# A transformer block in one core: when GpSimd sums the second weight set, in the first half of the feed-forward part

## The chip, the core and the metric

The kernel runs on one core of a Trainium2 chip. The metric is the device time of one launch in microseconds (us). The core has five engines, each with its own instruction queue that is worked off in order: TensorE (PE in the profile; PEld is its weight load, which overlaps with matmuls), VectorE (DVE), ScalarE (ACT), GpSimd (POOL) and SyncE (SP), which here only issues transfers. Engines wait for each other on semaphores. ScalarE issues transfers too.

## The reference

A block with adaptive layer norm: an attention part (32 heads of 18, four segments of 512 rows with a memory), then a feed-forward part. The change lies in the latter:

```python
h = _layernorm(x, axis=-1) * (1 + cb) + sb          # x: 2048 x 576
x = x + gb * _B_ref(h, B_w_gate, B_w_up, B_w_down)

def _B_ref(x, w_gate, w_up, w_down):                # 576 x 4608, 576 x 4608, 4608 x 576
    g = _silu(x @ w_gate)
    u = x @ w_up
    return (g * u) @ w_down
```

All in float32.

## The kernel before

The attention part takes up to some 660 us and is not touched. The feed-forward part runs in two halves, `t = 0` and `t = 1`, of 1024 rows each. In each half a loop goes over 18 pairs `p` of weight blocks (2 x 128 of the 4608 columns). Each pair has two sets `z`: 0 is gate, 1 is up. A set's product of a 2 x 2 block of operands is made from seven products instead of eight (sums and differences of blocks; `m` = 1 to 7), so a pair has 14 steps `k` (0 to 13), one product each. A product is seven float32r matmuls of 512 columns: operands are split in a high part (`wh`, a cast on ScalarE) and a low part (`wl`, the difference, on VectorE). The list of steps is `ZM`; the last product of a set, `m = 3`, stands in step 1 of the next set (k = 8 for gate, k = 1 of the next pair for up).

The order of instructions on every engine is the order in which the program records them (a manual schedule); tiles bring the waits. In one step the recording order is: casts of weights to come (`prep_w`), the splits on VectorE that belong to the casts of the step before (`later`), the product with what follows it (`step`, which calls `fin`), loads, casts of the 64-row remainder (`prep_r`), GpSimd's sums and products, stores, down-projection work, the cast of down weights (`prep_d`) and of activations (`prep_a`).

- **Weights.** `load_o` brings a set `O[p, z]` of 768 KB (first half) to one of two buffers. Four of its seven blocks must first be made by `sum_o`: four GpSimd instructions of 128 x 384. `prep_w` runs five products ahead (`PF = 5`), with nine buffers. In the first half `store_o` writes the four sums to DRAM, and the second half loads them ready made, so GpSimd has no work there.
- **Remainder.** `prep_r(0, p, z, part)` casts the remainder of three blocks (`part` 0) and of the four summed ones (`part` 1); `store_r` keeps it for the second half.
- **Down weights.** `load_d` brings 576 columns for two blocks to one buffer, `mul_d` multiplies them with `gbB` (two GpSimd instructions), `sum_d` makes four differences for the second half (GpSimd), `prep_d` casts, and a store to `wdD` at k = 12 frees the buffer.
- **Products' ends.** Bank A is written by m = 1, 6, 7 and 4 in turn, each adding to the last, so ScalarE's copies (to bank B, to `tb`, to `tc`) must be made before the next product on it. `fin` ends a block of the result: VectorE adds `tb` or `tc` to the bank (L1150 for gate, L1158 for up), ScalarE takes the silu (L1151, or L1148 straight from the bank), and the up set multiplies (L1155, L1159). `tb` and `tc` have one buffer each.
- **Down projection.** In the first half, `plain` adds one chunk of the pair before (12 matmuls of 288 columns into `pd`, two buffers) in each of the steps 4 to 11, and VectorE adds `pd` to the accumulator (L1260).
- **The second block's preparation.** In steps 2 to 11 of the first half a generator (`g2`, `prep2`) makes the other 1024 rows' operands, with small transfers on SP, casts on ScalarE and a few instructions on VectorE and GpSimd.

Per step of the first half, the touched order before: the load of the next pair's set 0 at k = 2 and of its set 1 at k = 12; `sum_o` of set 0 at k = 7, 8, 9, of set 1 in the next pair at k = 2, 3, 4; `mul_d` at k = 5, 6; `sum_d` at k = 6, 7, 9, 10.

Of the kernel before, what the change touches and what calls it, by code (L numbers as in the profile page):

```python
# [34 lines left out]
PF = 5  # L35
# [39 lines left out]
def block(ctx: ExitStack, tc: tile.TileContext, x, wqk, wv, wo, beta, wgu, wd, c, w_mod, out):  # L75
    nc = tc.nc
# [997 lines left out]
    def store_o(p, z):  # L1074
        nc.scalar.dma_start(oD[p][z], O[p, z][:, 3:7, 0:2])

    def prep_r(t, p, z, part=0):
        if part == 0:
            R[z] = wrp.tile([P, 7, P], F32R, tag="wr", name="wr")
        r = R[z]  # L1080
        if t == 1:
            (nc.sync if p or z == 0 else nc.scalar).dma_start(f32(r[0:96]), rD[p][z])
            return
        o, c = O[p, z], slice(0, 3) if part == 0 else slice(3, 7)
        nc.scalar.copy(r[0:96, c], o[0:96, c, 2, :])
        later.append(lambda: nc.vector.tensor_tensor(r[32:64, c], o[32:64, c, 2, :], f32(r[32:64, c]), op=ALU.subtract))

    def sum_o(p, z, j):
        o = O[p, z]
        d, a, b, op = ((4, 3, 2, ALU.add), (5, 4, 0, ALU.subtract), (3, 0, 3, ALU.subtract), (6, 1, 5, ALU.subtract))[j]  # L1090
        nc.gpsimd.tensor_tensor(o[:, d], o[:, a], o[:, b], op=op)  # L1091

    def store_r(p, z):
        nc.scalar.dma_start(rD[p][z], f32(R[z][0:96]))
# [17 lines left out]
    def mul_d(p, f):  # L1112
        v = RW[p][:, 2 * f:2 * f + 2].rearrange("p a b -> p (a b)")
        nc.gpsimd.tensor_tensor(v, v, gbB, op=ALU.mult)

    def sum_d(p, j):
        r = RW[p]
        d, a, b = ((4, 1, 0), (5, 3, 4), (6, 2, 5), (1, 3, 1))[j]
        nc.gpsimd.tensor_tensor(r[:, d], r[:, a], r[:, b], op=ALU.subtract)
# [17 lines left out]
                             skip_group_check=not first)  # L1137

    T, SG, AC, AP = {}, {}, {}, {}

    def tmp(tag, bufs=1):
        return tp.tile([P, L], F32, tag=tag, name=tag, bufs=bufs)

    def fin(z, ij, bank, add=None):
        if z == 0:
            SG[ij] = g = tmp("sg", NSG)
            if add is None:
                nc.scalar.activation(g, bank, AF.Silu)  # L1148
            else:
                nc.vector.tensor_tensor(g, bank, add, op=ALU.add)  # L1150
                nc.scalar.activation(g, g, AF.Silu)  # L1151
            return
        g = SG.pop(ij)
        if add is None:
            nc.vector.tensor_tensor(g, bank, g, op=ALU.mult)  # L1155
        else:
            u = tmp("cu", 2)
            nc.vector.tensor_tensor(u, bank, add, op=ALU.add)  # L1158
            nc.vector.tensor_tensor(g, u, g, op=ALU.mult)  # L1159
        AC[ij] = g  # L1160
# [114 lines left out]
    with tc.manual_schedule():  # L1275
# [101 lines left out]
        for t in range(2):  # L1377
            for p in range(NPR):
                last = t == 1 and p == NPR - 1
                nx = (p + 1) % NPR  # L1380
                tn = t if nx else t + 1
                if t == 0 and p == NPR - 1:
                    run(g2)
                    p6.close()
                    accq = pool(p4, "acq")
                    new_acc(accq, (1, 6, 7))
                if last:
                    load_x11(1)
                chunk = 0
                for k in range(14):  # L1390
                    z, m = ZM[k]
                    todo, later[:] = later[:], []
                    while nw < len(seq) and nw <= n + PF:
                        prep_w(*seq[nw])
                        nw += 1
                    n += 1
                    for f in todo:
                        f()
                    if k != 1 or prev is not None:
                        step(z, m)  # L1400
                    if k == 1 and prev is not None:
                        PA[0, 1] = AC[0, 1]
                    if t == 0 and p == NPR - 1 and k in (7, 9, 10, 11, 12, 13) or t == 1 and p == 0 and k == 1:
                        load_y(ACT_OP[m])
                    swap = t == 1 and p == 0
                    if not last and k == 7 - PF + swap:
                        load_o(tn, nx, 0)
                    elif not last and k == (14 - PF if tn else 12):
                        load_o(tn, nx, 1)
                    if t:  # L1410
                        if k == 2 + swap:
                            prep_r(1, p, 1)
                        elif not last and k == 9:
                            prep_r(1, nx, 0)
                    else:
                        if k in (3, 7):
                            prep_r(0, p, 1, k // 7)
                        elif tn == 0 and k in (9, 10):
                            prep_r(0, nx, 0, k - 9)
                        elif tn and k == 8:  # L1420
                            prep_r(1, 0, 0)
                        if k == 1:
                            load_d(0, p)
                        elif k in (2, 3, 4) and p:
                            for j in ((0, 1), (2,), (3,))[k - 2]:
                                sum_o(p, 1, j)
                        elif k in (5, 6):
                            mul_d(p, k - 5)
                        if tn == 0 and k in (7, 8, 9):
                            for j in ((0,), (1, 2), (3,))[k - 7]:  # L1430
                                sum_o(nx, 0, j)
                        if k in (6, 7, 9, 10) and p < NPR - 2:
                            sum_d(p, (6, 7, 9, 10).index(k))
                        if k == 0 and p == 0:
                            store_o(p, 0)
                        elif k == 3:
                            store_r(p, 0)
                        elif k == 6:
                            store_o(p, 1)
                        elif k == 10:  # L1440
                            store_r(p, 1)
                        elif k == 12:
                            nc.scalar.dma_start(wdD[p][:, :NS[p]], RW[p][:, :NS[p]])
                        elif k == 13 and tn == 0:
                            store_o(nx, 0)
                    if t and k == 2 + 2 * swap:
                        load_d(1, p)
                    if prev is not None and is_plain(*prev):
                        if k in (0, 2):
                            ij = (1, 0) if k == 0 else (0, 1)  # L1450
                            prep_a(prev[1] % 2, ij, PA[ij])
                        if CH0[t][k]:
                            f = plain(*prev, chunk)
                            if f:
                                late[k + 3] = f
                            chunk += 1
                        due(k)
                    elif prev is not None:
                        for j in range(4):
                            if k == KS[j]:  # L1460
                                sum_a(j)
                        if k == 0:
                            prep_a(prev[1] % 2, 2, PA[1, 0])
                        for j, kk in KA:
                            if k == kk:
                                prep_a(prev[1] % 2, j, PA[ASRC[j]])
                        for _ in range(CH[k]):
                            down(*prev, chunk)
                            chunk += 1
                    if last and 1 <= k < 9:  # L1470
                        comb(k - 1)
                    if p == 0 and (t, k) in RS:
                        load_res(t, RS[t, k])
                    if is_plain(t, p):
                        if k in (6, 7, 8, 10):
                            j = (6, 7, 8, 10).index(k)
                            prep_d(p, (j // 2, j % 2), j)
                    elif k >= 7:
                        prep_d(p, POS[k - 7], WSLOT[POS[k - 7]])
                    for ij, kk, j in (((0, 0), 11, 1), ((1, 1), 13, 4)):  # L1480
                        if k == kk:
                            prep_a(p % 2, ij if is_plain(t, p) else j, AC[ij])
                    if t == 0 and k in G2 and p > 0:
                        next(g2, None)
                for k in sorted(late):
                    due(k)
                PA.clear()
                PA.update(AC)
                prev = (t, p)
# [61 lines left out]
```

## Time and profile before

| | us |
|---|---|
| median of 3 runs | 1945.05 (1944.93 to 1948.55) |
| the profiled execution | 1944.18 |
| its span, first to last instruction | 1942.5 |
| TensorE busy | 1884.8 |
| VectorE busy | 1522.1 |
| ScalarE busy | 925.9 |
| GpSimd busy | 581.8 |

The prediction shows the profile's lines. They are read so: a window's row has start and end, length, then the busy time and the instructions of each engine, the granted clock of TensorE as a share of full speed, and the transfers. A group's row has the line, engine, operation, output and inputs, shape, count, busy time, mean in ns of one, and the idle time of the engine before them with what ended it. A row of waits has who waited for whom, the total, the number of times and the longest. A row of the timeline has start, length, engine, line, operation and count; in brackets stands idle time before it.

### The profile page before, as it was taken

To read this page: it belongs to the slowest core of one execution; us is meant where nothing else is said; L and a number is where in the kernel's file an instruction comes from. 1 tells how busy PE (TensorE), PEld (TensorE's weight loads), DVE (VectorE), ACT (ScalarE), POOL (GpSimd) and SP (SyncE) were. 2 spreads that over 40 slices of the span, in tenths; PEclk is the share of its full clock that TensorE was granted. 3 is DMA by queue.
4 is the path that set the end of the run, shared out by engine and by line. 5 is a ranking of instruction groups with operands and counts; after the bars stand their busy time and mean duration, and the time that the engine had idled before them with its cause. 6 is when DMAs were issued, how large, how long until landed. Compare 5 with 4: busy or idle time off the path is not lost.

```text
span 1942.5 us, 30570 instructions
## 1 busy us (share of the span) xinstructions
PE 1884.8 (97%) x10927; PEld 1568.8 (81%) x10927; DVE 1522.1 (78%) x3267; ACT 925.9 (48%) x2036; POOL 581.8 (30%) x772
## 2 busy tenths in 40 slices
PE   7999999999999799999999999999999999999999
PEld 4888865676766688888888888888888888888888
DVE  6485257878786899898778889876888888888887
ACT  2222256767666444444444444443444445454442
POOL 5222235555544645454345445310000000000000
PEclk9999999999999899999999999999999999999999
DMA  7767565444444555454445454369323333332331
GB/s 207 240 224 244 201 204 145 127 144 145 137 128 125 167 197 176 132 196 157 153 163 168 151 171 154 113 227 292 112 81 117 100 121 100 113 108 86 110 108 63
DMA packets 173543, 296.63 MB, mean 153 GB/s; under 512 B 25104, under 2 KB 101776, under 8 KB 171920
## 3 DMA queue, kind: packets, MB, share of 16 engines
q1 hardware_dynamic: 143280, 237.09, 39.0%
q10 hardware_dynamic: 30112, 57.60, 8.5%
q8 instruction: 86, 1.41, 0.3%
q14 instruction: 65, 0.53, 0.1%
HBM read 185.29 MB, written 109.31 MB: 152 GB/s over the span
## 4 chain that ended last, share of the span: by engine, by line
PE 84%; DVE 7%; DMA 5%; issue 1%; ACT 1%; POOL 1%; SPq 0%; ACTq 0%; DVEq 0%; POOLq 0%
PE A L1136 22%; PE pd L1256 13%; PE C L1136 10%; PE pd L1239 9%; PE B L1136 5%; PE pp L101 5%; PE s L589 4%; PE av L609 4%; PE s L187 4%; PE pv L101 3%; PE pw L707 2%; DVE wl L1101 1%; DMA mD<-mr 1%; DVE al L1200 1%; DVE y L938 1%
## 5 line engine op out<-in xcount | busy, mean ns | idle before, releaser
L1136 PE MATMUL A<-y,wh 128*128 128x512 f32 x1152 | 408.6, 395 | 10.1 <-ACT tb L1164 7.8
L192 DVE CUSTOM_DVE_ANT_0 junk<-s,tri 128x256 bf16<-128x256 f32 (+3 forms) x512 | 228.6, 487 | 76.5 <-PE s L187 67.9
L1101 DVE TENSOR_TENSOR wl<-O,wh 128x256 fp32r<-128x256 f32 x504 | 271.4, 540 | 5.4 <-ACT wh L1100 4.8
L1136 PEld LDWEIGHTS A<-y,wh 128*128 128x128 f32 x1152 | 217.7, 189 | 57.5 <-ACT tb L1164 11.0
L1091 POOL TENSOR_TENSOR O<-O 128x384 f32<-128x384 f32 x144 | 167.7, 1181 | 223.4 <-DMA O<-in_wgu_dram 75.0
L592 ACT ACTIVATE Pt<-s 128x512 f32<-128x512 f32 (+1 forms) x352 | 186.6, 558 | 87.3 <-PE s L589 72.7
L1136 PE MATMUL A<-y,wl 128*128 128x512 f32 x576 | 227.7, 395 | 0.0
L1244 DVE TENSOR_TENSOR acc<-acc,pd 128x576 f32<-128x576 f32 x216 | 162.3, 751 | 55.1 <-PE pd L1239 48.0
L1100 ACT CAST wh<-O 128x256 fp32r<-128x256 f32 x504 | 198.5, 404 | 11.5 <-DMA O<-in_wgu_dram 10.8
L1136 PE MATMUL C<-y,wh 128*128 128x512 f32 x576 | 202.5, 392 | 0.0
L1260 DVE TENSOR_TENSOR acc<-acc,pd 128x576 f32<-128x576 f32 x156 | 117.2, 751 | 98.6 <-PE pd L1256 97.9
L1256 PE MATMUL pd<-dh,ah 128*128 128x288 f32 x640 | 190.1, 297 | 4.3 <-DVE acc L1260 4.1
L1256 PE MATMUL pd<-dh,al 128*128 128x288 f32 x640 | 189.7, 296 | 0.0
L1256 PE MATMUL pd<-dl,ah 128*128 128x288 f32 x640 | 189.6, 296 | 0.0
L1200 DVE TENSOR_TENSOR al<-sg,ah 128x512 fp32r<-128x512 f32 x192 | 152.1, 792 | 12.1 <-ACT ah L1199 11.6
L1199 ACT CAST ah<-sg 128x512 fp32r<-128x512 f32 x192 | 118.7, 618 | 81.3 <-DVE sg L1159 79.6
L589 PE MATMUL s<-qs,ks 110*128 110x512 f32 (+2 forms) x384 | 149.8, 407 | 6.2 <-DMA qs<-mD 3.8
L1151 ACT ACTIVATE sg<-sg 128x512 f32<-128x512 f32 x73 | 46.2, 633 | 222.1 <-DVE sg L1150 222.1
L187 PE MATMUL s<-ks,qs 108*128 108x256 f32 (+3 forms) x512 | 141.3, 327 | 2.8 <-DMA ks<-kD 1.4
L1239 PE MATMUL pd<-dh,ah 128*128 128x288 f32 x448 | 133.0, 297 | 0.0
L1239 PE MATMUL pd<-dh,al 128*128 128x288 f32 x448 | 132.5, 296 | 0.0
L1239 PE MATMUL pd<-dl,ah 128*128 128x288 f32 x448 | 132.3, 295 | 0.0
(349 smaller groups left out, 4458.9 us busy)
## 6 DMA issues: line engine op xcount, KB each, us to landing
O<-in_wgu_dram SPq DMA_DIRECT2D x36, 768.0 KB
oD<-O ACTq DMA_DIRECT2D x36, 512.0 KB
O<-oD SPq DMA_DIRECT2D x36, 512.0 KB
ks<-kD SPq DMA_DIRECT2D x68, 216.0 KB
qs<-qD SPq DMA_DIRECT2D x68, 216.0 KB
O<-in_wgu_dram SPq DMA_DIRECT2D x36, 384.0 KB
rD<-wr ACTq DMA_DIRECT2D x36, 336.0 KB
wr<-rD SPq DMA_DIRECT2D x35, 336.0 KB
```

The lines of the kernel that those rows point to most:

```text
L187: nc.tensor.matmul(bank[:, n * (h - h0):n * (h - h0) + n], lhsT=qst[b][0:108, h, 128 * i:128 * i + 128], rhs=kst[b][0:108, h // 2, 0:n], s ...
L192: nc.vector.tensor_tensor_reduce(junk[:, :n], bank[:, n * (h - h0):n * (h - h0) + n], tri[:, L - n:], 1.0, -3e38, op0=ALU.add, op1=ALU.max ...
L589: nc.tensor.matmul(bank[:, n * (g - h):n * (g - h + w)].rearrange("p (a b) -> p a b", a=w), lhsT=kst[u % NB][0:110, g // 2, 128 * j:128 * ...
L592: nc.scalar.activation(pt[:, h:h + per, :n], bank[:, :n * per].rearrange("p (a b) -> p a b", a=per), AF.Exp, scale=SCALE)
L1091: nc.gpsimd.tensor_tensor(o[:, d], o[:, a], o[:, b], op=op)
L1100: nc.scalar.copy(wh, o)
L1101: later.append(lambda: nc.vector.tensor_tensor(wl, o, f32(wh), op=ALU.subtract))
L1136: nc.tensor.matmul(bank, lhsT=a, rhs=b, start=(first and n == 0), stop=(n == 6), skip_group_check=not first)
L1200: later.append(lambda: nc.vector.tensor_tensor(al, src, f32(ah), op=ALU.subtract))
L1239: nc.tensor.matmul(pd[:, i, :288], lhsT=a[:, tk], rhs=w, start=(k == 0), stop=(k == 2))
L1244: nc.vector.tensor_tensor(o, o, pd[:, :, :288], op=ALU.add)
L1256: nc.tensor.matmul(pd[:, i, :288], lhsT=a[:, tk], rhs=w, start=(k == 0), stop=(k == 5))
```

## The change

Five things move; no instruction is added or taken away.

1. The silu of L1151 is put off: it is recorded in the next step, behind that step's casts of weights and splits. This holds in both halves.
2. First half: the load of the next pair's set 1 moves from k = 12 to k = 8 (in the change's words, which count from 1: step 9). For this, step 7 casts two products' weights and step 8 none.
3. First half: set 1's sums move from k = 2, 3, 4 of their own pair to k = 10 and 11 of the pair before, two each; set 0's go from k = 7, 8, 9 to k = 4 to 7, one each.
4. `mul_d` goes one step earlier (k = 4, 5), `sum_d` stands at k = 6, 7, 8, 9, the first three `prep_d` one step earlier, and the second `prep_r` of set 1 at k = 5 and not 7.
5. Stores: the sums of set 0 at k = 11 (was 13), those of set 1 at k = 13 (was 6 of the next pair), the remainder of set 1 at k = 8 (was 10). Pair 0 stores both sets' sums at k = 0.

```diff
@@ fin
                 nc.vector.tensor_tensor(g, bank, add, op=ALU.add)
-                nc.scalar.activation(g, g, AF.Silu)
+                acts.append(lambda: nc.scalar.activation(g, g, AF.Silu))
@@ the loop over steps
-                    while nw < len(seq) and nw <= n + PF:
+                    while nw < len(seq) and nw <= n + PF + (t == 0 and k == 7):
                         prep_w(*seq[nw])
                         nw += 1
                     n += 1
                     for f in todo:
                         f()
+                    while acts:
+                        acts.pop(0)()
...
                     if not last and k == 7 - PF + swap:
                         load_o(tn, nx, 0)
-                    elif not last and k == (14 - PF if tn else 12):
+                    elif not last and k == (14 - PF if tn else 8):
                         load_o(tn, nx, 1)
...
-                        if k in (3, 7):
-                            prep_r(0, p, 1, k // 7)
+                        if k in (3, 5):
+                            prep_r(0, p, 1, k // 5)
...
                         if k == 1:
                             load_d(0, p)
-                        elif k in (2, 3, 4) and p:
-                            for j in ((0, 1), (2,), (3,))[k - 2]:
-                                sum_o(p, 1, j)
-                        elif k in (5, 6):
-                            mul_d(p, k - 5)
-                        if tn == 0 and k in (7, 8, 9):
-                            for j in ((0,), (1, 2), (3,))[k - 7]:
-                                sum_o(nx, 0, j)
-                        if k in (6, 7, 9, 10) and p < NPR - 2:
-                            sum_d(p, (6, 7, 9, 10).index(k))
+                        elif k in (4, 5):
+                            mul_d(p, k - 4)
+                        if tn == 0 and 4 <= k < 8:
+                            sum_o(nx, 0, k - 4)
+                        elif tn == 0 and k in (10, 11):
+                            sum_o(nx, 1, 2 * k - 20)
+                            sum_o(nx, 1, 2 * k - 19)
+                        if k in (6, 7, 8, 9) and p < NPR - 2:
+                            sum_d(p, k - 6)
                         if k == 0 and p == 0:
                             store_o(p, 0)
+                            store_o(p, 1)
                         elif k == 3:
                             store_r(p, 0)
-                        elif k == 6:
-                            store_o(p, 1)
-                        elif k == 10:
+                        elif k == 8:
                             store_r(p, 1)
+                        elif k == 11 and tn == 0:
+                            store_o(nx, 0)
                         elif k == 12:
                             nc.scalar.dma_start(wdD[p][:, :NS[p]], RW[p][:, :NS[p]])
                         elif k == 13 and tn == 0:
-                            store_o(nx, 0)
+                            store_o(nx, 1)
...
                     if is_plain(t, p):
-                        if k in (6, 7, 8, 10):
-                            j = (6, 7, 8, 10).index(k)
+                        if k in (5, 6, 7, 10):
+                            j = (5, 6, 7, 10).index(k)
                             prep_d(p, (j // 2, j % 2), j)
```

More of the change, by code (lines that the diff above doesn't have):

```diff
@@ L1139, in block @@
     T, SG, AC, AP = {}, {}, {}, {}
+    acts = []
     def tmp(tag, bufs=1):
```

## The prediction

> **What bounds the kernel now.** I read the page first, for the engine that is full, then the first half of the feed-forward part pair by pair, then who holds the matmuls up there, then the chain through one such hold.
>
> ```profile
> span 1942.5 us, 30570 instructions
> ...
> PE 1884.8 (97%) x10927; PEld 1568.8 (81%) x10927; DVE 1522.1 (78%) x3267; ACT 925.9 (48%) x2036; POOL 581.8 (30%) x772
> ```
>
> TensorE is busy for 97% of the span, and the change removes no matmul. All it can win is time in which TensorE stands still, or runs at half clock, in the part it touches. The next view cuts that part (659.7 to 1308.8 us) into its 18 pairs of weight blocks; I show a quiet one, the three worst and the sum.
>
> ```profile
> core 0: us, PE busy (x) PEld busy (x) DVE busy (x) ACT busy (x) POOL busy (x), PEclk, DMA share, GB/s
> ...
> 936.80:975.60 38.80, 36.41 (x203) 31.97 (x202) 29.27 (x44) 17.43 (x39) 18.16 (x17) 1.00 0.47 148
> 975.60:1015.20 39.60, 37.36 (x196) 32.37 (x195) 31.13 (x49) 17.15 (x41) 13.40 (x13) 0.96 0.40 129
> ...
> 1087.00:1122.40 35.40, 35.40 (x195) 31.17 (x194) 31.66 (x46) 16.40 (x39) 18.24 (x16) 1.00 0.55 165
> ...
> 1232.60:1273.40 40.80, 37.42 (x196) 32.30 (x195) 34.74 (x48) 16.79 (x41) 13.95 (x13) 0.96 0.41 132
> ...
> sum 649.10, PE 635.79 PEld 554.62 DVE 543.94 ACT 299.05 POOL 296.69; mean PE 35.32 PEld 30.81 DVE 30.22 ACT 16.61 POOL 16.48
> ```
>
> A quiet pair takes 35.4 us, with TensorE busy throughout. Three pairs take 3.4 to 5.4 us more. Over all 18 TensorE idles 649.1 - 635.8 = 13.3 us, and in two of the three bad pairs the granted clock falls to 0.96: 0.04 x 39.6 and 0.04 x 40.8, so 1.6 us each. The prize is thus about 16.5 us, under 1%. Who holds TensorE there, and after 1309 us:
>
> ```profile
> PE A L1136 <- ACT tb L1164: 7.8, 6, 2.4
> PE pd L1256 <- DVE acc L1260: 4.1, 2, 3.4
> PE A L1136 <- ACT cu L1164: 0.7, 1, 0.7
> PE pt L1036 <- DVE acc L1260: 0.5, 1, 0.5
> ```
>
> ```profile
> PE A L1136 <- DMA y<-yD: 1.5, 1, 1.5
> ```
>
> Mostly it is the copy of `tb` on ScalarE, which must clear bank A before the next product adds to it. The second half has no wait but one on a transfer. The chain through the hold at 943 us says what makes the copy late:
>
> ```profile
> 930.69 1.63 PE A L1136 x7
> 932.32 1.62 PE pd L1256 x12
> ...
> 935.31 1.42 DVE al L1200
> ...
> 939.92 1.34 DVE wl L1101
> 941.26 1.84 DVE al L1200
> ...
> 944.65 0.61 DVE cu L1158
> ...
> 945.36 0.59 ACT tb L1164
> ```
>
> The rows also give the steps (I count `k` from 0, as the loop does): 1.6 us for a product, 1.6 us more in steps 4 to 11, which carry down-projection work. So steps 12, 13 and 0 to 3 are short, 9.7 us for six, and steps 4 to 11 are long, 8 x 3.2 = 25.7 us. The chain runs through VectorE in the short steps: `cu` frees the one `tb` buffer, and stands behind `wl` and `al` that take 1.3 to 1.8 us. GpSimd is at work at that very time:
>
> ```profile
> 934.00 5.04 POOL L1091 TENSOR_TENSOR O<-O 128x384 f32<-128x384 f32 x4 [7.72 <-DVE dl L1126]
> 939.55 3.01 POOL L1114 TENSOR_TENSOR dr__11734<-dr__11734,gbB 128x576 f32<-128x576 f32 x2 [0.52 <-DMA dr__11734<-in_wd_dram]
> 942.51 1.25 POOL L1119 TENSOR_TENSOR dr__11734<-dr__11734 128x288 f32<-128x288 f32 x1
> ```
>
> That GpSimd makes VectorE slow is seen by comparing the first half (first fence, 684 to 1309 us) with the second, where GpSimd does nothing:
>
> ```profile
> L1101 DVE TENSOR_TENSOR wl<-O,wh 128x256 fp32r<-128x256 f32 x239 | 158.7, 667 | 2.8 <-ACT wh L1100 2.3
> L1260 DVE TENSOR_TENSOR acc<-acc,pd 128x576 f32<-128x576 f32 x136 | 102.1, 751 | 81.3 <-PE pd L1256 80.6
> L1200 DVE TENSOR_TENSOR al<-sg,ah 128x512 fp32r<-128x512 f32 x69 | 67.7, 981 | 3.9 <-ACT ah L1199 3.4
> L1086 DVE TENSOR_TENSOR wr<-O,wr 32x384 fp32r<-32x384 f32 x66 | 52.3, 793 | 2.5 <-ACT wr L1085 0.5
> ...
> L1158 DVE TENSOR_TENSOR cu<-C,tb 128x512 f32<-128x512 f32 x17 | 11.6, 680 | 0.0
> ```
>
> ```profile
> L1101 DVE TENSOR_TENSOR wl<-O,wh 128x256 fp32r<-128x256 f32 x224 | 93.7, 418 | 0.0
> L1200 DVE TENSOR_TENSOR al<-sg,ah 128x512 fp32r<-128x512 f32 x112 | 76.8, 686 | 4.4 <-ACT ah L1199 4.4
> ...
> L1126 DVE TENSOR_TENSOR dl<-dr__18260,dh 128x288 fp32r<-128x288 f32 x7 | 3.2, 453 | 0.0
> ```
>
> `wl` has a mean of 667 ns against 418, `al` 981 against 686. Last, the short steps at the start of a pair in which GpSimd happened to be almost idle, and at that of two bad ones:
>
> ```profile
> 717.80:727.49 9.69, 9.69 (x45) 7.96 (x44) 9.24 (x18) 4.02 (x10) 1.02 (x1) 1.00 0.91 320
> ...
> 933.57:945.80 12.23, 10.04 (x45) 7.92 (x43) 11.77 (x13) 3.90 (x10) 9.18 (x7) 1.00 0.46 165
> 972.40:984.99 12.59, 10.35 (x46) 7.95 (x45) 12.10 (x14) 4.08 (x11) 8.91 (x8) 1.00 0.46 162
> ```
>
> Even with GpSimd idle VectorE is busy 9.24 of 9.69 us there: it has no room. With 9 us of GpSimd work, one of its instructions takes 0.86 to 0.91 us instead of 0.51, and TensorE pays.
>
> **The change part by part.** *The second set's load and sums.* Today the load of the next pair's second set stands on SP's queue behind all transfers of steps up to 11, and behind the last split of the buffer it overwrites. It starts late:
>
> ```profile
> 720.11 0.91 SPq L1069 DMA_DIRECT2D O<-in_wgu_dram  x1
> ```
>
> ```profile
> 726.33 0.41 ACT L1100 CAST wh<-O 128x256 fp32r<-128x256 f32 x1 [1.85 <-DMA O<-in_wgu_dram]
> ```
>
> That one was issued in step 13 (717.80 is the start of step 12), and the cast of step 2 waited for it: 726.3 less 720.1 to 721.0 is 5.3 to 6.2 us of landing. With the last cast of the old set in step 7, its split in step 8, and the load in step 8 ahead of that step's other transfers, it lands by 5.3 to 6.2 us, so in step 10. The four sums (5.04 us in the row above) then run in steps 10 and 11 and not in 12 to 4. Nothing queues behind the load on SP but small transfers of the second block's preparation. On GpSimd only such work of steps 10 and 11 queues behind the sums.
>
> *The first set's sums and the products with `gbB`.* The multiply comes first (step 4), then the sums alternate with the rest in steps 4 to 9. The first sum waits for the load issued in step 2 or 3, which by the same 5.3 to 6.2 us lands in step 5, and now has the second multiply behind it. That one is needed by the cast of step 7, so the 6.4 us of steps 5 and 6 cover its 1.3 + 1.5 us. The first multiply may run from the landing of its weights, at 939.55 in the row above, which was step 1: about half of 3.01 us stays in the short steps, against some 9 us now. VectorE loses on it at the rate below 0.8 us, and has 0.4 us of room, so it is some 0.4 us late once a pair. I price that at nothing to 0.5 us a pair, and take 0.05, since pairs that carry more GpSimd work than that there show no wait.
>
> *What steps 4 to 11 then hold.* VectorE has 8 `wl` x 0.418, 8 evictions x 0.751, 4 `dl` x 0.453, 4 `wr` x at most 0.793 and 4 others x 0.68: 17.0 us of 25.7. GpSimd gets 18 less 1.6, about 16 us. What does a microsecond of GpSimd cost VectorE? From the short steps: (0.905 - 0.513) x 13 / 9.18 and (0.864 - 0.513) x 14 / 8.91, both 0.55. From the long steps of another pair:
>
> ```profile
> 1021.60:1047.00 25.40, 25.40 (x151) 22.95 (x150) 21.73 (x31) 11.51 (x27) 13.69 (x12) 1.00 0.48 150
> ```
>
> (21.73 - 17.0) / 13.69 = 0.35. I take 0.35, since it comes from the same steps: 17.0 + 5.6 = 22.6 of 25.7 us, and TensorE waits for nothing, as in that row. The other end, 0.55, makes 25.8, just full. So the work hides behind TensorE, and the cover ends at (25.7 - 17.0) / 16 = 0.54. The evictions, for which TensorE waits there, keep 751 ns in both cases, for one of their inputs is in PSUM.
>
> The Trainium skill (SBUF — State Buffer, "Who interferes with whom") has a rule that speaks against the move: a VectorE instruction with two SBUF inputs and a GpSimd one that reads SBUF exclude each other, and whichever starts second waits for the whole of the other. The rows agree on who suffers (`wl`, `al`) and who doesn't (the evictions, `cu`). By that rule alone the 16 splits of steps 4 to 11 could each wait up to one sum of 1.26 us, 20 us in all and 11 us a pair too many; with GpSimd there 62% of the time and half an instruction left on average it is 16 x 0.62 x 0.63 = 6.3 us, which fits again.
>
> *Silus one step later.* ScalarE stands in these silus now:
>
> ```profile
> ACT sg L1151 <- DVE sg L1150: 133.4, 37, 9.0
> ```
>
> The cast of the next step now goes first. The result is read in the second set's steps, seven or more later, so nothing waits for it. In the first pair, where the casts that stood between silu and `tb` copy (0.4 us each) get out of the way, 0.8 us of a 1.1 us wait goes. In the second half, where TensorE never waits for ScalarE, it costs nothing.
>
> *Casts of `wr` and `dh` earlier, an extra cast in step 7, stores moved.* As many instructions as before. ScalarE is busy 16 to 17 us of 35.4, and casts stand five steps (8 to 16 us) ahead of their product. The store of the second set in step 13 makes ScalarE wait for the sums; landing early in step 10 plus 5.0 us is the end of step 11, and a copy TensorE needs comes only in step 0. This costs nothing unless the load is 3 us late.
>
> *The sum.* Two of the waits on `tb` fall in pairs 0 and 1 (659.5 to 693 us):
>
> ```profile
> PE A L1136 <- ACT tb L1164: 2.1, 2, 1.1
> ```
>
> Of the 7.8 us I keep 1.0 (pair 1: pair 0 has no down work, so its steps are too short for load and sums to finish in time) and 0.3 in pair 0: gain 6.5, and 1.6 for the half clock at 985 us. The waits on evictions (4.6 us, and 1.6 of half clock) come from another cause:
>
> ```profile
> 1241.24 6.54 DVE L999 TENSOR_TENSOR st<-t,st 32x256 fp32r<-32x256 f32 x1
> ```
>
> GpSimd ran without a break there, and one VectorE instruction got no turn. That may happen again in the new order; I count half, 3.1. Less 16 x 0.05 = 0.8. Together 6.5 + 1.6 + 3.1 - 0.8 = 10.4 us. The profiled execution took 1944.18 us (1.7 beyond its span), 0.9 below the median: 1933.8, and 1934.6 by the median. I say 1934.
>
> **The rivals.** *Everything goes.* If the new order also gives every VectorE instruction its turn, all but the 0.7 us at the first copy is won: 13.3 - 0.7 + 3.2 = 15.8, so 1929. For it: quiet pairs have no wait at all. Against: the single 6.54 us stall.
>
> *The wait moves.* The load is on time, but the lag that VectorE collects in steps 10 and 11 reaches `cu` in step 1 after all, or the load still stands behind a transfer and the sums stay where they are. Then dense waits remain and the time is 1945. For it: the short steps have 0.4 us of room. Against: a lag of one sum is well below the one that nine us of GpSimd work makes.
>
> *Slower: steps 4 to 11 overflow.* One mechanism: GpSimd's unbroken row of work in steps 5 to 8 and 10 to 11 costs VectorE over 0.54 us per us, evictions come late, and TensorE waits for one of the two `pd` buffers. At 0.60, 17.0 + 9.6 = 26.6, 0.9 us too many in 16 pairs, 14 us, with no gain left: 1959. For it: 0.55 was measured, and the 6.54. The Trainium skill's rule from above leads here, if a sum always starts just ahead of a split. Against: the pair with 13.69 us of GpSimd in these steps, and none waiting.
>
> **How the numbers follow.** Forecast 0.50, everything goes 0.25, the wait moves 0.11, overflow 0.14. About 0.2% (3.9 us) is what can be told from no change here. So faster 0.75, same 0.11, slower 0.14. The range goes from 1927 (all waits, and what the pairs lose beside them) to 1946, which takes in the unmoved case and leaves out the overflow.
>
> **What would show it.** Right: sums of the second set in steps 10 and 11; no wait of bank A on `tb` beyond the first two pairs; pairs at 35.4 to 36 us; `al`, which falls in the short steps, back near 690 ns; the first half some 10 us shorter, and the second unchanged. Wrong: waits of `pd` on `acc` in many pairs (overflow), second-set sums after step 12, ScalarE standing in the store of step 13, or the clock falling in other pairs.

## The result and the profile after

| | before | after |
|---|---|---|
| median, us | 1945.85 (4 runs, 1944.93 to 1948.55) | 1928.95 (4 runs, 1926.12 to 1931.29) |
| ratio, 95% interval | | 0.991 (0.9893 to 0.9928) |
| the profiled execution | 1944.18 | 1926.12 |

The kernel is 16.9 us faster, 14 to 21 us by the interval. The profiled execution of after is the fastest of its four.

The page of after:

```profile
span 1924.3 us, 30622 instructions
...
PE 1874.0 (97%) x10927; PEld 1562.5 (81%) x10927; DVE 1512.8 (79%) x3267; ACT 929.8 (48%) x2036; POOL 581.0 (30%) x772
```

The 18 pairs of the first half, as windows; I show pair 1, the pairs that were the worst (8, 9 and 16), the quiet one (12) and the sum:

```profile
core 0: us, PE busy (x) PEld busy (x) DVE busy (x) ACT busy (x) POOL busy (x), PEclk, DMA share, GB/s
...
680.10:719.20 39.10, 36.27 (x196) 31.02 (x195) 33.93 (x54) 15.75 (x37) 20.98 (x20) 1.00 0.50 170
...
933.20:969.70 36.50, 36.42 (x204) 31.96 (x203) 30.38 (x44) 17.46 (x39) 17.64 (x16) 1.00 0.48 156
969.70:1005.00 35.30, 35.30 (x196) 31.19 (x194) 30.82 (x46) 17.14 (x41) 18.01 (x16) 1.00 0.52 172
...
1076.70:1112.10 35.40, 35.40 (x196) 31.17 (x195) 31.60 (x46) 16.54 (x39) 16.96 (x15) 1.00 0.55 176
...
1220.40:1255.80 35.40, 35.40 (x195) 31.21 (x194) 29.40 (x47) 17.14 (x41) 13.86 (x12) 1.00 0.46 152
...
sum 635.70, PE 630.83 PEld 552.91 DVE 533.61 ACT 301.03 POOL 295.34; mean PE 35.05 PEld 30.72 DVE 29.64 ACT 16.72 POOL 16.41
```

GpSimd does the same work (295 us, as before), yet pairs 8, 9 and 16 are down from 38.8, 39.6 and 40.8 us, and the clock stands at 1.00 in all three. The sum is 13.4 us smaller. TensorE idles 635.7 - 630.8 = 4.9 us in it, where it was 13.3. Pair 1 got longer: 39.1 us, where it was 36.9. The waits of TensorE, from 655 to 1300 us, and then to the end:

```profile
PE A L1136 <- ACT B L1182: 1.8, 1, 1.8
PE C L1136 <- DVE cu L1159: 1.0, 1, 1.0
PE A L1136 <- ACT tb L1165: 1.0, 1, 1.0
PE A L1136 <- ACT cu L1165: 0.7, 1, 0.7
```

```profile
PE A L1136 <- DMA y<-yD: 0.8, 1, 0.8
```

All four of the first fence lie in pairs 0 and 1. GpSimd's timeline of pair 8 shows the new places (the pair starts at 933.2; its steps 4, 10 and 12 start at 939.6, 959.6 and 966.5):

```profile
937.65 1.43 POOL L1114 TENSOR_TENSOR dr__11739<-dr__11739,gbB 128x576 f32<-128x576 f32 x1 [6.24 <-DVE cu L1159]
945.75 1.02 POOL L1091 TENSOR_TENSOR O<-O 128x384 f32<-128x384 f32 x1 [6.67 <-DVE sg L1151]
...
952.87 2.87 POOL L1119 TENSOR_TENSOR dr__11739<-dr__11739 128x288 f32<-128x288 f32 x3
960.43 4.42 POOL L1091 TENSOR_TENSOR O<-O 128x384 f32<-128x384 f32 x4 [4.69 <-issue]
```

The second set's sums run in steps 10 and 11, one product with `gbB` is left in the short steps, and the rest stands in steps 5 to 8. The short steps of pairs 8 and 9, and the VectorE groups of the first half:

```profile
929.95:939.64 9.69, 9.69 (x45) 7.95 (x44) 9.11 (x15) 4.14 (x10) 2.89 (x3) 1.00 0.78 275
966.49:976.17 9.68, 9.68 (x45) 7.96 (x45) 9.07 (x15) 4.74 (x13) 2.13 (x2) 1.00 0.79 277
```

```profile
L1101 DVE TENSOR_TENSOR wl<-O,wh 128x256 fp32r<-128x256 f32 x239 | 149.9, 637 | 0.6 <-POOL dr__9794 L1114 0.3
L1261 DVE TENSOR_TENSOR acc<-acc,pd 128x576 f32<-128x576 f32 x136 | 101.9, 749 | 73.0 <-PE pd L1257 73.0
L1086 DVE TENSOR_TENSOR wr<-O,wr 32x384 fp32r<-32x384 f32 x66 | 60.8, 921 | 2.6 <-ACT wr L1085 0.7
L1201 DVE TENSOR_TENSOR al<-sg,ah 128x512 fp32r<-128x512 f32 x69 | 50.9, 738 | 4.9 <-ACT ah L1200 4.6
```

TensorE works through the windows at the short steps without a break, though VectorE is still busy for nearly all of them. In pairs 2 to 15 GpSimd is busy for 2.2 us of the six short steps on average, where it was 4.3. The hold on VectorE has moved rather than gone: `al`, which falls in the short steps, is down from 981 to 738 ns, `wr`, which falls in the long ones, is up from 793 to 921. The evictions keep their 750 ns.

### The profile page after: what moved, and what is told of

The parts are those of the page before. It is cut to its first block, busy times and chain, and to the rows that moved or that the text cites. A ratio compares the mean times of both kernels' runs of the same rounds, so it can differ in the third digit from the quotient of the medians.

```text
span 1924.3 us, 30622 instructions
## 1 busy us (share of the span) xinstructions
PE 1874.0 (97%) x10927; PEld 1562.5 (81%) x10927; DVE 1512.8 (79%) x3267; ACT 929.8 (48%) x2036; POOL 581.0 (30%) x772
## 4 chain that ended last, share of the span: by engine, by line
PE 88%; DMA 5%; DVE 4%; POOL 1%; issue 1%; ACT 1%; SPq 0%; ACTq 0%; POOLq 0%; DVEq 0%
PE A L1136 23%; PE pd L1257 13%; PE C L1136 12%; PE pd L1240 9%; PE B L1136 6%; PE s L589 4%; PE av L609 4%; PE pp L101 4%; PE s L187 4%; PE pv L101 3%; PE pw L707 2%; DMA y<-yD 1%; DMA mD<-mr 1%; PE pn L778 1%; DVE y L938 1%
## 5 line engine op out<-in xcount | busy, mean ns | idle before, releaser
L1101 DVE TENSOR_TENSOR wl<-O,wh 128x256 fp32r<-128x256 f32 x504 | 261.7, 525 | 4.2 <-ACT wh L1100 3.5
L1091 POOL TENSOR_TENSOR O<-O 128x384 f32<-128x384 f32 x144 | 163.3, 1146 | 179.1 <-DMA O<-in_wgu_dram 76.0
L1201 DVE TENSOR_TENSOR al<-sg,ah 128x512 fp32r<-128x512 f32 x192 | 135.2, 704 | 8.8 <-ACT ah L1200 8.4
L1257 PEld LDWEIGHTS pd<-dl,ah 128*128 128x128 f32 x640 | 120.5, 188 | 7.1
```

The lines of the kernel that those rows point to most:

```text
L1101: later.append(lambda: nc.vector.tensor_tensor(wl, o, f32(wh), op=ALU.subtract))
L1201: later.append(lambda: nc.vector.tensor_tensor(al, src, f32(ah), op=ALU.subtract))
L1257: nc.tensor.matmul(pd[:, i, :288], lhsT=a[:, tk], rhs=w, start=(k == 0), stop=(k == 5))
```

## The experiments

Pair times here are read from the timeline, from the first product of a pair to that of the next. Pairs 2 to 14 are the part that all extra loads below leave free of side effects.

| run | median, us | ratio to before (95%) | pairs 0, 1 | pairs 2 to 14 | pairs 2 to 17 |
|---|---|---|---|---|---|
| before | 1945.85 | | 61.3 | 474.3 | 587.8 |
| after | 1928.95 | 0.991 (0.9893 to 0.9928) | 63.3 | 464.4 | 572.3 |
| after_again | 1928.36 | 0.9886 (0.9868 to 0.9905) | 63.2 | 464.4 | 572.0 |
| silu_only | 1944.98 | 0.999 (0.9976 to 1.0004) | 60.5 | 473.3 | 586.7 |
| no_silu | 1927.12 | 0.9906 (0.9889 to 0.9922) | 63.2 | 464.2 | 571.7 |
| load_only | 1939.99 | 0.9964 (0.9948 to 0.9981) | 63.7 | 468.8 | 579.8 |
| set1_back | 1937.93 | 0.9959 (0.9946 to 0.9972) | 60.9 | 467.8 | 582.3 |
| short_read | 1944.19 | 1.0 (0.9983 to 1.0017) | 63.4 | 468.2 | 586.4 |
| short_write | 1941.13 | 0.9986 (0.9968 to 1.0003) | 65.0 | 464.5 | 584.5 |
| long_read | 1931.35 | 0.9949 (0.9934 to 0.9964) | 63.0 | 465.1 | 574.3 |
| short_read14 | 1933.36 | 0.9914 (0.9893 to 0.9935) | 64.6 | 469.1 | 576.7 |
| short_write14 | 1928.36 | 0.989 (0.9868 to 0.9912) | 63.1 | 464.4 | 572.1 |
| pair0 | 1925.89 | 0.9917 (0.9899 to 0.9935) | 58.8 | 464.4 | 572.1 |
| pair0_again | 1925.69 | 0.987 (0.9851 to 0.9889) | 61.1 | 464.3 | 571.9 |

The ratios go against runs of before in the same series, whose median was 1947.46, 1944.26 and 1950.6 us in the three series. Before ran 54 times in all, from 1937.0 to 1954.6 us, and the changed kernel 8 times, from 1926.1 to 1931.3; the columns of pairs come from one profiled execution each. The part ahead of the first product, which no edit touches, took 655.8 to 661.9 us in these profiles; so runs are compared by their pairs where a few us matter.

**Is it the silu?** The theory was that GpSimd's sums in the short steps hold VectorE, and so the copy; the rival, that ScalarE standing in the silu makes the copies late. One run does the silu alone, one undoes it.

```diff
+                acts.append(lambda: nc.scalar.activation(g, g, AF.Silu))     # silu_only: this part alone
-                acts.append(lambda: nc.scalar.activation(g, g, AF.Silu))     # no_silu: this part undone
+                nc.scalar.activation(g, g, AF.Silu)
```

> The kernel before with the silu of L1151 put off by one step and nothing else. Theory (GpSimd's sums in the short steps hold VectorE, and so the tb copy): the gain is 0 to 2 us, 1944 to 1946 us, waits of bank A on tb stay at 5 us or more in pairs 1 to 17. Rival (ScalarE standing in the silu is what makes the copies late): 10 us or more are won, 1936 us or less, and the waits on tb are gone.

> The changed kernel with the silu put back where it was. Theory: at most 2 us are lost, 1929 to 1931 us, no waits on tb in pairs 2 to 17. Rival (silu): 10 us or more are lost, 1939 us or more.

The silu alone gives 0.999, an interval that holds 1. Without it the changed kernel is as fast. The waits in silu_only, from 655 to 1300 us, are still there:

```profile
PE pd L1257 <- DVE acc L1261: 6.2, 3, 3.4
PE A L1136 <- ACT tb L1165: 5.6, 5, 2.5
```

ScalarE does stand less in the silu (110.7 us for 133.4), but nothing waited for that. In no_silu one wait on `tb` in pair 0 is 3.3 us where the changed kernel has 1.0, and the clock falls there; pair 1 gives as much back. The rival falls.

**Which half of the move?** One run takes the earlier load alone, with the sums still recorded in steps 2 to 4 of the next pair. The other undoes the second set's load, sums and store in the changed kernel.

```diff
# load_only, against before
-                    while nw < len(seq) and nw <= n + PF:
+                    while nw < len(seq) and nw <= n + PF + (t == 0 and k == 7):
...
-                    elif not last and k == (14 - PF if tn else 12):
+                    elif not last and k == (14 - PF if tn else 8):
# set1_back, against after: both of these undone, and
+                        if k in (2, 3, 4) and p:
+                            for j in ((0, 1), (2,), (3,))[k - 2]:
+                                sum_o(p, 1, j)
...
-                        elif tn == 0 and k in (10, 11):
-                            sum_o(nx, 1, 2 * k - 20)
-                            sum_o(nx, 1, 2 * k - 19)
...
-                            store_o(p, 1)                    # in step 0 of pair 0
+                        elif k == 6:
+                            store_o(p, 1)
...
-                        elif k == 13 and tn == 0:
-                            store_o(nx, 1)
```

> The kernel before with the load of the second set in step 8 (and its extra cast in step 7), the sums recorded where they were, in steps 2 to 4 of the next pair. GpSimd's queue holds nothing between its differences of step 10 and these sums, so they run when the data has landed. Theory (when the data lands decides when the sums run, not the place in the text): sums in steps 10 to 12, most of the gain, 1930 to 1936 us. Rival (the place of the sums in the order decides): sums still in steps 0 to 4, 1943 to 1946 us.

> The changed kernel with the second set's load, sums and store back in their old places; the silu, the first set's sums, the products with gbB, the differences and the down casts stay moved. Theory: the gain goes nearly whole, 1940 to 1946 us, with waits on tb in several pairs. Rival (the first set's sums and the earlier down work brought the gain): 1929 to 1934 us.

Neither theory's numbers came: each of the two wins about half, 7.5 and 9.5 us by the medians, 8.0 and 5.5 us in pairs 2 to 17, of 15.5. The sums of load_only do run when the data lands, in steps 10 to 12 of most pairs, so the place in the text does not decide alone. But it decides where another GpSimd instruction stands in front. GpSimd in load_only, around the start of pair 3 (759.2; step 12 of pair 2 starts at 756.0):

```profile
755.14 0.67 POOL L1015 TENSOR_TENSOR rs<-rs,mhalf 128x1 f32<-128x1 f32 x1 [5.29 <-DVE rs L1014]
755.78 4.75 POOL L1091 TENSOR_TENSOR O<-O 128x384 f32<-128x384 f32 x4
762.78 1.42 POOL L1114 TENSOR_TENSOR dr__9789<-dr__9789,gbB 128x576 f32<-128x576 f32 x1 [2.26 <-DVE wl L1101]
```

By the 4.1 to 4.7 us that the others of this run took, the load had landed in step 10; the sums queued behind the preparation's `rs` of step 11 and fell into the short steps again, and pair 3 lost 1.6 us in its first five steps. In other pairs the free GpSimd did both products with `gbB` and a difference in steps 1 to 4. So the first set's edits matter too: with the first sum between the two products, the second product cannot come early.

Set1_back keeps a wait of another kind, in pair 16. Its VectorE and its TensorE wait:

```profile
1232.27 9.39 DVE L999 TENSOR_TENSOR st<-t,st 32x256 fp32r<-32x256 f32 x1
```

```profile
PE pd L1257 <- DVE acc L1261: 4.8, 1, 4.8
```

GpSimd beside it:

```profile
1229.52 2.17 POOL L1091 TENSOR_TENSOR O<-O 128x384 f32<-128x384 f32 x2 [13.56 <-DVE wl L1101]
...
1238.49 2.88 POOL L1091 TENSOR_TENSOR O<-O 128x384 f32<-128x384 f32 x3
```

It is the VectorE instruction that took 6.54 us in before; in silu_only it took 6.55, in after 0.42. In all three slow cases it stood beside GpSimd work that ran without a break from step 3 on.

**Is it the reads, and is it the place?** Extra GpSimd work that nothing uses goes into the changed kernel: sums that read SBUF, or memsets that only write it, in the short steps; and the same sums in a long one.

```diff
+        jk = pool(p4, "jk").tile([P, 288], F32, tag="jk", name="jk")
...
+                    if t == 0 and 0 < p < NPR - 1 and k == 13:              # short_read, short_write
+                        a = AC[1, 1][:, 0:1]
+                        nc.gpsimd.tensor_tensor(jk[:, 0:1], a, a, op=ALU.add)
+                        for _ in range(8):                                  # short_write: 22
+                            nc.gpsimd.tensor_tensor(jk, gbB[:, :288], gbB[:, :288], op=ALU.add)
+                            nc.gpsimd.memset(jk, 0.0)                       # short_write, in place of the sum
...
+                            for _ in range(8 if k == 4 and p > 1 else 0):   # long_read, behind the first mul_d
+                                nc.gpsimd.tensor_tensor(jk, gbB[:, :288], gbB[:, :288], op=ALU.add)
```

> The changed kernel with extra GpSimd work in the short steps, whose result nothing reads: after step 13 of pairs 1 to 16 eight sums of 128 x 288 from SBUF (some 0.8 us each, 6.4 us), started by the end of the block of step 12. Theory (GpSimd's reads in the short steps hold VectorE): the waits on tb come back, 0.7 to 3 us a pair, 1939 us or more. Rival (only the late data mattered, a busy GpSimd does no harm by itself): 1929 to 1932 us.

> The same place and about the same GpSimd time, but 22 memsets of 128 x 288 (some 0.3 us each), which read nothing. Theory of a shared read path: VectorE is not held, 1927 to 1932 us, wl near 420 ns in the short steps. Rival (any GpSimd work there, or the order behind it on GpSimd, does harm): as slow as the run with sums.

> The changed kernel with the same eight sums, but in the long steps: after the first product with gbB in step 4 of pairs 2 to 17, where GpSimd has idle time until the first set's load lands. Theory (the long steps have room for it): 1927 to 1933 us, no new waits. Rival (the amount of GpSimd work counts, not its place): as slow as in the short steps, or waits of pd on acc.

By their times the first two are both slow, and short_write seems to go against the theory. The pairs tell why: of what pairs 2 to 17 lose against after (14.1 and 12.2 us), 7.9 and 11.4 us lie in pair 17 alone (43.5 and 47.0 us), where the rest of the preparation is run out, a cast on ScalarE waits for a GpSimd instruction, and that had queued behind my extra work. So both were run again with the work in pairs 1 to 13 only.

> As short_read, but the extra sums only in pairs 1 to 13, since in pair 17 a cast on ScalarE stood behind a GpSimd instruction that queued behind them, 7.6 us. Theory (GpSimd's reads hold VectorE): 1933 to 1938 us, waits on tb in most of pairs 2 to 14, al and wl in the short steps longer than 690 and 420 ns. Rival (that queue made the whole loss): 1928 to 1931 us.

> As short_write, but the memsets only in pairs 1 to 13. Theory (memsets read nothing, so VectorE is not held): 1928 to 1931 us, pairs 2 to 14 as short as in the changed kernel. Rival (any GpSimd work in the short steps): as slow as short_read14.

VectorE's `al` between 720 and 1150 us, with the sums and then with the memsets:

```profile
L1201 DVE TENSOR_TENSOR al<-sg,ah 128x512 fp32r<-128x512 f32 x48 | 57.7, 1203 | 0.0
```

```profile
L1201 DVE TENSOR_TENSOR al<-sg,ah 128x512 fp32r<-128x512 f32 x49 | 33.7, 687 | 7.9 <-ACT ah L1200 7.7
```

Sums of about 6.8 us (8 x 0.81 and a small one) make `al` 1203 ns and pairs 2 to 14 4.7 us longer, and TensorE waits for `tb` in four of them (I had expected it in most):

```profile
PE A L1136 <- ACT tb L1165: 1.7, 4, 0.6
```

Counted from the start of each matmul to the next, the product of step 4, which needs `tb` out of the way, loses 4.2 of the 4.7 us, over half of it in delays too short to show as a wait; with the memsets it loses 0.2. Memsets of 7.8 us (22 x 0.34 and the same small one) leave `al` at 687 ns, no wait of TensorE in that stretch, and the pairs at 464.4 us, as without them. So it is GpSimd's reads that hold VectorE, not its being busy. The Trainium skill (SBUF — State Buffer, "Who interferes with whom") states that a VectorE instruction with two SBUF inputs is in the way of GpSimd's reads and not of its writes; these two runs agree. The memsets do make GpSimd late: right behind them its products and sums ran without a break, and one `wl` beside them took 4.16 us (short_write14, pair 14, step 6), one 6.92 us (short_write, pair 16, step 5). TensorE waited for the second, 0.9 us.

The same sums in step 4 cost pairs 2 to 14 0.7 us, and pairs 2 to 17 2.0, of which a wait for a transfer of the preparation makes 1.1:

```profile
PE pt L1036 <- DMA xb<-xh: 1.1, 1, 1.1
PE pd L1257 <- DVE acc L1261: 0.6, 1, 0.6
```

So the place counts more than the amount. Put together over the pairs 2 to 17 of seven runs (before, after_again, silu_only, load_only, set1_back, short_read14, pair0_again), the first five steps of a pair take over 9.65 us by this much, against GpSimd's busy time from step 12 to the start of step 3:

```
GpSimd, us   pairs   mean excess, us   largest
0 to 4          80              0.17      2.39
4 to 6          29              0.66      1.67
6 to 7.5         3              3.24      4.27
```

(The 0.17 is mostly transposes of the preparation, which some of these steps hold. The 4.27 us, of before, have 1.7 us of half clock in them. The amount alone does not decide: the 2.39 us are load_only's pair 16, where the two products with `gbB` ran in a row in steps 2 and 3, 3.0 us, and held one `wl` and one `al` for 1.65 and 1.92 us; TensorE waited 1.6 us for `tb` there.)

**What is left in pairs 0 and 1.** The chain of waits in after, from 680 to 690 us:

```profile
679.60 1.20 POOL O L1091
680.80 0.07 issue
680.87 3.91 POOL O L1091 x3
684.78 0.02 issue
684.80 0.52 ACTq L1075
685.32 0.04 issue
685.36 0.62 ACT ah L1200
685.98 0.30 ACT wh L1100
686.29 0.49 ACT B L1182
```

ScalarE stands in the store of step 13 until the four sums are done, in steps 0 to 2 of pair 1, and the copy to bank B comes late. The mended version:

```diff
-                        elif k in (4, 5):
+                        elif k in (4, 5) and p:
                             mul_d(p, k - 4)
+                        elif k == 4:
+                            mul_d(p, 0)
+                            mul_d(p, 1)
+                            for j in range(3):
+                                sum_d(p, j)
...
-                        if k in (6, 7, 8, 9) and p < NPR - 2:
+                        if k in (6, 7, 8, 9) and p < NPR - 2 and (p or k == 9):
...
-                        elif k == 13 and tn == 0:
+                        elif k == 6 and p == 1:
+                            store_o(p, 1)
+                        elif k == 13 and tn == 0 and p:
                             store_o(nx, 1)
```

> The changed kernel with the first pair mended: in pair 0 both products with gbB and three of the differences run before the first set's sums, and the store of the second set's sums moves to step 6 of pair 1, so ScalarE need not stand in it. If the waits left in pairs 0 and 1 (1.0 on tb, 1.0 on cu, 1.8 on the copy to bank B) come from GpSimd being late there, 2 to 4 us are won against the changed kernel: 1925 to 1927 us. If they come from the load being late, nothing is won.

> The changed kernel again, on the same chip as the others of this call: 1926 to 1931 us.

> The kernel with the first pair mended again, beside the changed kernel: its pairs 0 and 1 were 4.5 us shorter in the profile, so 3 to 5 us below the changed kernel.

Pairs 0 and 1 take 58.8 and 61.1 us in its two profiles, for 63.3 and 63.2 us, and the medians are 1925.9 and 1925.7 for 1929.0 and 1928.4. Of the 4.5 us between the first profiles 1.0 is the granted clock, which still ran at half into pair 0 in after and had recovered in pair0; in the second profiles this is equal (0.9 us each), and 2.1 us are left. The medians of the last series differ by 2.7 us, a little less than the 3 to 5 expected, and the intervals of its two ratios overlap (0.9851 to 0.9889 and 0.9868 to 0.9905), so the gain, 2 to 3.5 us, rests on the pairs. The wait on the copy to bank B falls from 1.8 to 0.3 us. By its medians it beats both kernels.

## Why the prediction was right, and where it was off

- **The place and the mechanism were right.** TensorE had waited for `tb`, that for `cu`, that for splits held by GpSimd. The reads in the short steps were shown to do it (sums against memsets), and their place, by the sums in step 4.
- **The landing was right.** From the issue of the second set's load (its start or its end) to the first sum that waited for it were 3.9 to 5.6 us in after, somewhat less than the 5.3 to 6.2 I took, and the sums run from step 10 on. The 9 us of GpSimd work that I gave to the short steps before were those of the worst pairs; the mean is 4.3.
- **The long steps have room, as forecast.** No `pd` wait on `acc` is left. In pairs 2 to 15 VectorE is busy for 21.3 us of steps 4 to 11 on average, with 15.5 us of GpSimd work, where I had 22.6 and 16. The overflow rival fell, with another 6.5 us of sums in them too: one wait of 0.6 us.
- **The silu was right to be left out of the main gain,** by two runs. For pair 0 I had counted 0.8 us of a wait on `tb` to it; with the silu alone that wait is 0.8 us for 1.1, and in after it is 1.0, so most of it stayed.
- **What was mis-sized: the waits on evictions.** I counted half of 4.6 us and 1.6 us of half clock as won (3.1), taking the 6.54 us stall for a matter of turns that may come again in the new order. All of it went. The stall was no accident: it fell on the same instruction in three kernels, 6.5, 6.55 and 9.4 us, each time as the second set's sums, late, ran straight on into the products and the first set's sums. In after, after_again, no_silu and both runs of the mended kernel no VectorE instruction of the first half takes over 2 us. But the new order alone does not rule such a stall out: where memsets made GpSimd late, stalls came back (4.16 and 6.92 us).
- **What was mis-sized the other way: pairs 0 and 1.** I kept 1.0 and 0.3 us on `tb` there and priced the store of step 13 at nothing unless the load were 3 us late. In pair 0, whose steps have no down work, the sums are as late as that, and TensorE waits 3.8 us in pairs 0 and 1 beside the first copy's 0.7. ScalarE standing in that store was one of my signs of being wrong, and it came, in this one pair.
- **Two smaller terms.** The 0.8 us that I took off for the product left in the short steps did not show: pairs 2 to 17 have no wait. The signs came nearly as named: `al` is at 738 ns and not near 690, and pairs 2 to 17 are at 35.3 to 36.8 us, those above 36 all with transposes of the preparation in them (204 TensorE instructions for 196).
- **The sum.** Over the 18 pairs, 10.4 us were forecast and 13.4 measured: 8.4 us less idle, 3.2 of half clock, and 1.8 that no wait in the view names. Matmuls of 512 columns start 0.23 us apart and their records last 0.40, so up to 0.16 us of a wait is in no view; before has ten waits in these pairs and after four, which makes some 1.0 of the 1.8. The rest stays open. Of the 18.1 us between the two profiled executions, 3.9 lie ahead of the first product, in code that didn't change, and go with that run; 0.7 are a shorter wait for `y`. The time came out at the rival in which everything goes (1929), though not by its own sum, since pairs 0 and 1 lost; that my 1934 is as near as it is, is partly luck, for the terms that were off go both ways.

## What to carry to other kernels

Ask of helper work on GpSimd when it runs, not only how much it is: its reads hold VectorE's instructions with both inputs in SBUF, and here that cost time mostly where VectorE had no room, in the six steps without down work. An in-order engine runs its work when the data has landed and the instruction ahead is done, so the second set's load moved by itself won about half, the first set's sums and the products moved by themselves won another half, and only the whole move kept the work out of these steps. No run moves the recorded place of the second set's sums alone. A store that waits for a late producer holds everything behind it on its queue, so look at the first turn of a loop, which is shorter, by itself.

## What the runs showed of the hardware

- A VectorE instruction of 32 x 256 waited through seven to nine GpSimd instructions in a row (6.5 and 9.4 us), and one of 128 x 256 through six (4.16 and 6.92 us); in before all others that were held, but one, lost under 1.5 us. What decides the turn stays open.
- The granted clock changed only on a grid of 3.41 us. Taken stretch by stretch over the first halves of the fourteen profiles, each of the ten stretches at full clock in which TensorE stood still for 1.79 us or more was followed by one at half clock; none with 1.65 us or less was, and of three with 1.78 us one. So the wait of 2.24 us at 982 us in before, which lies in one stretch, cost half clock, and that of 2.38 us at 943 us, which falls half in one stretch and half in the next, did not.
- Memsets on GpSimd, 7.5 us a pair, left VectorE's `al` at 687 ns, where it is 686 in the second half of before, with GpSimd idle.
